# Attention plus gated MLP with its backward pass: dead buffers take wo's last rows and two O^T tiles, w_down is loaded in pieces, the guard's end and the first row tiles get a fixed place

## The chip, the cores and the metric

The kernel runs on one core of a Trainium2 chip. The number that counts is the device time in microseconds of one execution; the kernel before has a median of 5105.49 us over six runs (5099.11 to 5111.01). Lower is better. The core has a matrix engine (PE, TensorE), a vector engine (DVE), a scalar engine (ACT), a general engine (POOL, GpSimd) and a sync engine (SP), each with an instruction stream of its own. SP and POOL here mostly issue DMA transfers, each from its own queue and in the order of that queue.

## The reference

One layer, and the gradients of its inputs. With S = 2048 rows, D = 576, H = 32 heads of 128, F = 4608:

```python
xn = layernorm(x)                                   # per row
q  = (xn @ wq)  per head                            # keys and values come from caches
p  = softmax(q k^T * 128 ** -0.5)
s  = concat_heads(p @ v) @ wo
h  = sigmoid(xn @ w_gate) * (xn @ w_up)
out = x + s * silu(h @ w_down)
# returned: out and the gradients of x, k_cache, v_cache, wq, wo, w_gate, w_up, w_down
```

All tensors are bfloat16; sums are kept in float32.

## The kernel before, in words

Rows are cut into NT = 16 tiles of 128, D into five contraction tiles (DT), F into 36 (FT). The work is one long sequence of stages.

*Stage a1, norm and the first half of the MLP (lines 305 to 435).* `x_all` holds all rows. For each tile, `bn` (DVE) takes statistics, `rstd` (ACT square root, then DVE) turns those of several tiles into scale and bias, `norm` (ACT) normalizes in place, `turn` (PE) transposes into PSUM and `put_T` copies into `xnT`, the transposed xn, which is kept for the heads' queries. The weights of gate and up are loaded in five column groups (`groups1`: one of 512 columns, four of 1024). The loop runs over groups and in each over the 16 row tiles; for every 512 columns PE makes `g_ps` (L408) and `u_ps` (L410), ACT the sigmoid into `a_row` (L413), DVE the product into `h_row` (L414). `a_row` and `h_row` have four buffers each; POOL stores both per row tile (L427, L428), and a buffer is free again when its store has landed. In group 0 the norms and transposes of later tiles run two tiles ahead. After group 0 POOL stores xn (L430) and loads w_down whole (L431).

This stage lies in `tc.manual_schedule()`: on each engine the instructions written in the block keep the written order. Elsewhere a planner decides at build time, from its own estimate of when each instruction is ready, so an instruction may stand far from where it is written; instructions written after the block can also be put between those of the block.

*The guard.* `guard_load` (SP) and `guard_square` (DVE and ACT in turn) sum squares of the keys and of wq through the dead `x_all`, to choose between two softmax forms. `guard_reduce` sends two columns through DRAM into `gr`; `guard_end` (L299 to L303, five short DVE instructions) makes the flag. It is called after the block of a1.

*Stage a2 (lines 442 to 513)* multiplies h by w_down (L486), makes silu and its derivative, and transposes the gradient of s into `dsT`.

*The heads (lines 540 to 796).* Each head has 16 slots of scores (`main1`: L578, exponent L596) and 16 of gradients (`main2`: L648, L651), with work of neighbouring heads between them. `put(slot, ...)` writes a piece of work into a slot; the planner orders what is written. SP transposes every slab of probabilities (`PT`) and of their gradient (`dST`, both L572), wanted by PE (L625) five slots later. Sums over queries (L684) leave as `kvo` tiles (L696) with two buffers, stored by POOL (L698). O is stored to `on2_d` four row tiles at a time. In the last head, rows of wo are loaded into buffers that are no longer needed (`wo_parts`: dsT takes 17 heads' rows, one K buffer, V and dO three each; 26 of 32), and O^T of the first row tile goes into the dead K^T/Q^T buffer `KQ` (L532).

*Stage c1, output projection (lines 839 to 902).* The other six heads' rows of wo are loaded into `wo_x` at its start. For each row tile SP transposes that tile's rows of `on2_d` (L532) into one of two buffers (`KQ`, `oTb`), one tile ahead; PE runs 64 matmuls (L887); ACT and DVE make the gradient `doB` and the output tile `o0b`. Every two row tiles POOL loads the next `dsg`, `g2b`, `xb` and stores `o0b`. PE transposes each `doB` tile (L58) about two row tiles later. From row tile 12 on, POOL loads `ah` and SP pieces of w_down^T for the next stage. Here SP and POOL keep the written order, and memory of dead tiles is waited for tile by tile.

*The rest (stages b1, c2, c4)* makes the weight gradients and the gradient of x. `xn_all` is reloaded in b1 (L958).

Of the kernel before, what the change touches and what calls it, by code (L numbers as in the profile page):

```python
# [13 lines left out]
P = 128  # L14
# [52 lines left out]
def kernel(  # L67
# [160 lines left out]

    px = tc.alloc_tile_pool(name="px", bufs=1)
    xnT = px.tile([P, DT, S], bf, name="xnT")  # L230
    flag_i = pers.tile([1, 1], mybir.dt.int32, name="flag_i")
    with tc.tile_pool(name="pa", bufs=1) as pa:
# [75 lines left out]
        with tc.tile_pool(name="a1w", bufs=1) as wp:  # L308
# [30 lines left out]
            with tc.tile_pool(name="a0", bufs=3) as sb0, tc.tile_pool(name="a0ps", bufs=2, space=PSUM) as ps0, \  # L339
# [39 lines left out]
                for st in range(LA):  # L379
                    norm(st)  # L380
                    turn(st)
                    put_T(st, "v")
                for st in range(LA, L1):
                    bn(st)
                if LA < L1:
                    rstd(LA, L1)
                    norm(LA)
                bn_left = list(range(L1, NT))
                nstep = sum(NT * (fz - fa) for fa, fz in groups1[1:])
                ntot = len(pieces) + GLA  # L390
                step = 0
                for gi, (fa, fz) in enumerate(groups1):
                    for st in range(NT):
                        if gi == 0:
                            if st + LA + 1 < NT:
                                norm(st + LA + 1)
                            if st + LA < NT:
                                turn(st + LA)
# [3 lines left out]
                        for fc in range(fa, fz):  # L402
# [6 lines left out]
                            for i, (d0, kd) in enumerate(dts):  # L409
                                nc.tensor.matmul(u_ps[:], lhsT=xnT[:, i, srows], rhs=wu_sb[:, i, fs], start=(i == 0), stop=(i == DT - 1))  # L410
                            if gi == 0 and st + LA < NT:
                                put_T(st + LA, "s")
                            nc.scalar.activation(a_row[:, cs], g_ps[:], AF.Sigmoid)  # L413
# [13 lines left out]
                        nc.gpsimd.dma_start(h_d[srows, fa * FCH:fz * FCH], h_row[:, :nn])  # L427
                        nc.gpsimd.dma_start(a_d[srows, fa * FCH:fz * FCH], a_row[:, :nn])  # L428
                    if gi == 0:
                        nc.gpsimd.dma_start(xn_d[:, :].rearrange("(t p) d -> p t d", p=P), x_all[:])  # L430
                        nc.gpsimd.dma_start(wd_sb[:], B_w_down.rearrange("(t p) d -> p t d", p=P))  # L431
            while gk[0] < ntot:
                guard_step()
                if gk[0] == ntot:
                    guard_reduce()
            guard_end()
            NHV = min(NT, NT * D // (FT * P))
# [77 lines left out]
        gp.release()  # L515

    wo_parts = []
    for dead, t_ in enumerate((dsT, Kns[H % 2], Vn, dOn)):
        flat = t_[:].rearrange("p a b -> p (a b)")
        h0 = sum(n for _, _, n, _ in wo_parts)  # L520
        n = min(flat.shape[1] // D, H - h0)
        if n:
            wo_parts.append((flat[:, :n * D].rearrange("p (h d) -> p h d", d=D), h0, n, dead))
    n_pre = sum(n for _, _, n, _ in wo_parts)

    def load_wo_rows(dst, h0, a, b, eng=nc.gpsimd):
        eng.dma_start(dst[:, a:b, :], A_wo[(h0 + a) * P:(h0 + b) * P, :].rearrange("(h p) d -> p h d", p=P))

    oT0 = KQ[:].rearrange("p a b -> p (a b)")[:, :H * P].rearrange("p (h q) -> p h q", q=P) if H * P <= 2 * S else None

# [9 lines left out]
    def attention(fast):  # L540
        with ExitStack() as es:
# [184 lines left out]
            def q(k):  # L726
                return min(k, NT - 1)
# [46 lines left out]
            for view, h0, n, dead in wo_parts:  # L774
                for k in range(0, n, 4):
                    at = (1 + k // 4, q(skew + 1), q(skew + 2), q(skew + 4))[dead]
                    put(bl + q(at), 0, lambda view=view, h0=h0, k=k, n=n: load_wo_rows(view, h0, k, min(k + 4, n)))
            if oT0 is not None:
                put(bl + NT, 0, lambda: load_oT(oT0, 0))
            slot = 0  # L780
# [19 lines left out]
    pdT.release()  # L800
    px.release()

# [11 lines left out]
    with late("pc") as pc, late("pcw") as pcw, late("pcf") as pcf, \  # L814
# [23 lines left out]

        with late("c1w") as wp, late("c1b") as blk, late("c1l3", 2) as ldp3, late("c1s", 2) as sb, \
                late("c1ps", 2, space=PSUM) as ps, late("c1pt", 2, space=PSUM) as pst:  # L840
            wo_of = {}
            for view, h0, n, _ in wo_parts:
                for k in range(n):
                    wo_of[h0 + k] = view[:, k, :]
            if n_pre < H:
                wo_x = wp.tile([P, H - n_pre, D], bf, name="wo_x")
                load_wo_rows(wo_x, n_pre, 0, H - n_pre)
                for k in range(H - n_pre):
                    wo_of[n_pre + k] = wo_x[:, k, :]
            oTs = [oT0 if oT0 is not None else blk.tile([P, H, P], bf, name="oTa")[:], blk.tile([P, H, P], bf, name="oTb")[:]]  # L850
            if oT0 is None:
                load_oT(oTs[0], 0)
            SG1 = ldiv(NT, 2)
# [12 lines left out]
            for st in range(NT):  # L866
                if st + 1 < NT:
                    load_oT(oTs[(st + 1) % 2], st + 1)
                g, sl = divmod(st, SG1)
                if sl == 0:  # L870
                    if g + 1 < NG1:
                        groups[g + 1] = group_loads(g + 1)
                    dsg, g2b, xb = groups.pop(g)
                    o0b = ldp3.tile([P, SG1, D], bf, name="o0b")
                if st >= NT - 2 - DT and len(wd_pieces) > (F // WCH - 1) * DT:
                    wd_piece()
                if st == NT - NT // 4:
                    load_blk(ah0[:, 0, :, :], a_d, 0)
                    load_blk(ah0[:, 1, :, :], h_d, 0)
                while len(pend_tr) > 1:  # L880
                    st_ = pend_tr.pop(0)
                    transpose_to(nc, pst, doB[:, st_, :], D, doBT, st_ * P, ident, alt, eng="s")
                oT = oTs[st % 2]
                accs = [ps.tile([P, 512], f32, name=f"acc{j}") for j in range(len(ncs))]
                for h in range(H):
                    for j, (n0, nn) in enumerate(ncs):
                        nc.tensor.matmul(accs[j][:, :nn], lhsT=oT[:, h, :], rhs=wo_of[h][:, n0:n0 + nn],  # L887
                                         start=(h == 0), stop=(h == H - 1))
                s_sb = sb.tile([P, D], f32, name="s_sb")
                for j, (n0, nn) in enumerate(ncs):  # L890
                    alt.copy(s_sb[:, n0:n0 + nn], accs[j][:, :nn], eng="s")
                nc.vector.tensor_tensor(doB[:, st, :], s_sb[:], dsg[:, sl, :], op=ALU.mult)
                t0 = sb.tile([P, D], f32, name="t0")
                nc.vector.tensor_tensor(t0[:], s_sb[:], g2b[:, sl, :], op=ALU.mult)
                nc.vector.tensor_tensor(o0b[:, sl, :], t0[:], xb[:, sl, :], op=ALU.add)
                if sl == SG1 - 1:
                    nc.gpsimd.dma_start(o0[g * SG1 * P:(g + 1) * SG1 * P, :].rearrange("(t p) d -> p t d", p=P), o0b[:])
                pend_tr.append(st)
            while len(wd_pieces) > (F // WCH - 1) * DT:
                wd_piece()  # L900
            for st_ in pend_tr:
                transpose_to(nc, pst, doB[:, st_, :], D, doBT, st_ * P, ident, alt, eng="s")
        pds.release()

        def padded(pool, n, nm):
# [255 lines left out]
```

## Time and profile before

| | us |
|---|---|
| profiled execution, its own time | 5110.69 |
| its span, first to last instruction | 5108.8 |
| median of six runs (lowest, highest) | 5105.49 (5099.11, 5111.01) |
| PE busy in the span | 4989.5 |
| stage a1 | 0 to 360 |
| stage a2 | 360 to 512 |
| heads | 512 to 3704 |
| output projection c1 | 3706 to 3850 |
| rest | 3850 to 5109 |

The mean granted clock of PE is 0.992. Times in the profile are microseconds from the start of the span unless marked ns. A row of the timeline gives start, duration, engine, source line, operation and the tiles written and read; the bracket is how long the engine had been idle before it and which instruction or transfer ended that. A wait row gives the waiter, the releaser, the sum of the waits, their number and the longest. In a table of stretches each row gives the stretch, its length, PE busy time with its number of matmuls, the granted clock, the DMA share and GB/s. A busy PE is not a PE at full speed: after a pause its clock can be half, and five matmuls of 512 columns then take 2.1 us instead of 1.08.

### The profile page before, as it was taken

The page shows a single profiled execution, that of the slowest core. Times are in us where ns is not written, and L with a number is a line of the kernel's source. Part 1 is how long each engine was busy: PE and PEld are TensorE (multiplying, and loading weights), DVE is VectorE, ACT ScalarE, POOL GpSimd, SP SyncE. Part 2 cuts the span into 40 slices and gives each one's busy share as a digit, 9 for nine tenths or more (in the row PEclk, how much of TensorE's full clock was granted, in tenths as well). Part 3 has the DMA queues.
Part 4 walks back from the last instruction along what each step waited for, and adds up shares of the span by engine and source line. Part 5 has one row for each costly group of instructions (what it writes and reads, how often), then busy time and mean ns, then how long its engine had stood idle before and what let it go on. Part 6 is the DMA issues. An engine that isn't in the chain of part 4 may idle for free.

```text
span 5108.8 us, 128905 instructions
## 1 busy us (share of the span) xinstructions
PE 4989.5 (98%) x54480; PEld 3487.2 (68%) x54480; DVE 2583.3 (51%) x6704; ACT 2574.2 (50%) x4634; POOL 928.8 (18%) x1434
## 2 busy tenths in 40 slices
PE   7999999999999999999999999999999999999999
PEld 3445777787777777777777777777746666555554
DVE  4544666666566666666665666665525444200111
ACT  4431766676666666666666666666513333211000
POOL 3222111111111111111111111111112222211000
PEclk9999999999999999999999999999999999999999
DMA  8667999999999999999999999999996665797976
GB/s 285 219 182 171 212 205 204 200 210 217 193 201 209 215 203 209 198 207 207 209 208 196 205 213 205 208 201 195 214 214 192 190 188 185 221 260 187 175 141 121
DMA packets 2761921, 1031.37 MB, mean 202 GB/s; under 512 B 2664497, under 2 KB 2668722, under 8 KB 2761330
## 3 DMA queue, kind: packets, MB, share of 16 engines
q1 hardware_dynamic: 2660354, 699.97, 74.3%
q0 software_dynamic: 100976, 323.05, 19.5%
q8 instruction: 428, 7.01, 0.6%
q14 instruction: 163, 1.34, 0.1%
HBM read 175.31 MB, written 182.13 MB: 70 GB/s over the span
## 4 chain that ended last, share of the span: by engine, by line
PE 82%; issue 9%; DMA 6%; POOL 2%; DVE 2%; ACT 1%; POOLq 0%; SPq 0%; DVEq 0%; ACTq 0%
PE acc L684 14%; PE acc L625 14%; PE acc L916 13%; PE sp L578 8%; PE acc L1087 7%; PE dp L648 6%; PE acc L213 5%; PE dh L969 3%; PE acc L486 3%; PE g_ps L408 2%; PE u_ps L410 2%; DMA out_dram<-kvo 2%; PE acct L146 2%; PE acc L887 1%; DVE Pq L651 1%
## 5 line engine op out<-in xcount | busy, mean ns | idle before, releaser
L596 ACT ACTIVATE Pq<-sp 128x1024 bf16<-128x1024 f32 x1024 | 1047.0, 1023 | 317.0 <-PE sp L578 304.8
L684 PEld LDWEIGHTS <-Pq 128*128 128x128 bf16 x16384 | 1006.6, 98 | 242.1 <-issue 3.9
L655 ACT ACTIVATE t<-dp,negdelta 128x1024 bf16<-128x1024 f32 x512 | 571.1, 1115 | 222.6 <-PE dp L648 210.0
L651 DVE SCALAR_TENSOR_TENSOR Pq<-dp,negdelta,Pq 128x1024 bf16<-128x1024 f32 x512 | 655.3, 1280 | 44.3 <-PE dp L648 43.4
L648 PE MATMUL dp<-VT,dOT 128*128 128x512 bf16 x2048 | 613.9, 382 | 41.9 <-DVE Pq L651 41.8
L578 PE MATMUL sp<-KQ 128*128 128x512 bf16 x2048 | 610.1, 380 | 2.6 <-ACT Pq L596 2.5
L625 PEld LDWEIGHTS <-PT 128*128 128x128 bf16 x8192 | 502.4, 98 | 127.9 <-DMA PT<-Pq 7.0
L625 PE MATMUL acc<-Kn,dST 128*128 128x128 bf16 x8192 | 552.0, 219 | 5.6 <-DMA dST<-Pq 5.6
L625 PE MATMUL acc<-Vn,PT 128*128 128x128 bf16 x8192 | 547.5, 219 | 5.6 <-DMA PT<-Pq 5.4
L684 PE MATMUL acc<-dOn,Pq 128*128 128x128 bf16 x8192 | 547.0, 219 | 0.0
L684 PE MATMUL acc<-Qn,Pq 128*128 128x128 bf16 x8192 | 544.6, 220 | 0.0
L625 PEld LDWEIGHTS <-dST 128*128 128x128 bf16 x8192 | 492.8, 98 | 68.5 <-DMA dST<-Pq 8.1
L656 DVE TENSOR_TENSOR Pq<-t,Pq 128x1024 bf16<-128x1024 bf16 x512 | 354.3, 692 | 359.6 <-ACT t L655 352.9
L665 ACT ACTIVATE dq_n<-acc,rsc 128x128 bf16<-128x128 f32 x512 | 188.0, 367 | 340.1 <-PE acc L625 339.0
L1103 DVE SCALAR_TENSOR_TENSOR junk<-acc,xn_all 128x512 f32<-128x512 f32 (+1 forms) x32 | 13.9, 453 | 638.1 <-ACT dxn L1102 638.1
L698 POOL DMA_DIRECT2D out_dram<-kvo x256 | 140.3, 548 | 1062.8 <-DVE kvo L696 1062.8
L619 POOL DMA_DIRECT2D on_d<-o_n x128 | 97.0, 758 | 742.3 <-DVE junk L637 391.1
L971 DVE TENSOR_TENSOR du_blk<-dh,ah 128x256 bf16<-128x256 f32 x288 | 120.6, 419 | 191.5 <-PE dh L969 189.5
L696 DVE SCALAR_TENSOR_TENSOR kvo<-acc,part 128x512 bf16<-128x512 f32 x256 | 176.0, 688 | 76.0 <-DMA out_dram<-kvo 46.4
L1102 ACT ACTIVATE dxn<-acc 128x512 f32<-128x512 f32 (+1 forms) x32 | 12.8, 406 | 395.1 <-PE acc L1087 387.6
L648 PEld LDWEIGHTS <-dOT 128*128 128x128 bf16 x2048 | 163.9, 98 | 69.5 <-issue 47.5
L583 DVE TENSOR_REDUCE rs_all<-rsp 128x1 f32<-128x2 f32 x512 | 78.1, 153 | 256.0 <-ACT Pq L596 253.9
(200 smaller groups left out, 6956.5 us busy)
## 6 DMA issues: line engine op xcount, KB each, us to landing
out_dram<-kvo POOLq DMA_DIRECT2D x256, 128.0 KB, 4.1
ah<-a_d POOLq DMA_DIRECT2D x18, 1024.0 KB, 7.2
ah<-h_d POOLq DMA_DIRECT2D x18, 1024.0 KB, 9.6
du_d<-du_blk POOLq DMA_DIRECT2D x18, 1024.0 KB, 8.5
dg_d<-dg_blk POOLq DMA_DIRECT2D x18, 1024.0 KB, 10.1
h_d<-h_row POOLq DMA_DIRECT2D x64, 256.0 KB, 2.7
a_d<-a_row POOLq DMA_DIRECT2D x64, 256.0 KB, 3.5
x_all<-in_A_k_cache_dram SPq DMA_DIRECT2D x64, 256.0 KB, 3.6
```

Source lines behind the costliest of these rows:

```text
L213: nc.tensor.matmul(av[:, :CH], lhsT=w[:, i, :], rhs=srcT[:, i, cs], start=(i == 0), stop=(i == DT - 1))
L578: nc.tensor.matmul(sp[:, c * CH:(c + 1) * CH], lhsT=hs.QT[:, qt * P:(qt + 1) * P], rhs=hs.KT[:, hf * HW_ + c * CH: hf * HW_ + (c + 1) * CH ...
L596: nc.scalar.activation(Pq[:, hsl], sp[:], AF.Exp, scale=SCALE, accum_out=hs.rsp[:, hf:hf + 1])
L625: nc.tensor.matmul(hs.acc[:, 0, :], lhsT=T[:, kt, :], rhs=rhs[:, kt, :], start=(kt == 0), stop=(kt == NT - 1))
L648: nc.tensor.matmul(dp[:, c * CH:(c + 1) * CH], lhsT=hs.dOT[:, qt * P:(qt + 1) * P], rhs=hs.VT[:, hf * HW_ + c * CH: hf * HW_ + (c + 1) * C ...
L651: nc.vector.scalar_tensor_tensor(Pq[:, hsl], dp[:], hs.negdelta[:, qt:qt + 1], Pq[:, hsl], op0=ALU.add, op1=ALU.mult)
L655: nc.scalar.activation(t[:], dp[:], AF.Identity, bias=hs.negdelta[:, qt:qt + 1], scale=1.0)
L656: nc.vector.tensor_tensor(Pq[:, hsl], t[:], Pq[:, hsl], op=ALU.mult)
L665: nc.scalar.activation(hs.dq_n[:, qt % G4, :], hs.acc[:, 0, :], AF.Copy, scale=hs.rsc[:, qt:qt + 1])
L684: nc.tensor.matmul(self.tile[:, j, :], lhsT=self.slabs[qt][:, kt * P:(kt + 1) * P], rhs=self.rhs[:, qt, :], start=(qt == self.lo), stop=(q ...
L916: nc.tensor.matmul(accs[j][:, :nn], lhsT=lhs[:, st, cols], rhs=rhs[:, st, n0:n0 + nn], start=(st == 0), stop=(st == NT - 1))
L1087: nc.tensor.matmul(self.accs[sl][j][:, :nn], lhsT=ch[:, kk, sl * P:(sl + 1) * P], rhs=wT[:, k0 + kk, n0:n0 + nn], start=(self.k + kk == 0) ...
```

## The change

- `xnT` moves to the other end of SBUF and stays allocated until the end of c1. It is dead once the last head's queries are made. It takes wo's last six heads' rows and, behind them, O^T of row tile 1. `wo_x` and `oTb` are gone.
- O^T gets three buffers: `KQ`, the one in `xnT`, and one in `xn_all`, which is not yet filled in c1. Row tiles 0 and 1 are loaded in the heads' slots, 2 at the start of c1, and tile st + 2 during tile st.
- The output tile is written in place into `xb`; `o0b` is gone.
- w_down is loaded in twelve pieces of three F tiles, after the stores of every second row tile from column group 2 on; xn is stored in four pieces.
- `guard_end` is called inside the block whose order is fixed, after its last row tile.
- First row tiles: put_T of tile 1 goes to ACT; statistics and `rstd` of tiles 2 to 6 are split into 2, 3 and 4 to 6, with the norms of 2 and 3 after the first part; tile 2 is transposed after row 0's matmuls instead of before.

```diff
-    px = tc.alloc_tile_pool(name="px", bufs=1)
+    px = tc.alloc_tile_pool(name="px", bufs=1, side="right")
...
-                    put_T(st, "v")
-                for st in range(LA, L1):
-                    bn(st)
-                if LA < L1:
-                    rstd(LA, L1)
-                    norm(LA)
+                    put_T(st, "vs"[st % 2])
+                for a, b in ((LA, min(LA + 2, L1)), (min(LA + 2, L1), L1)):
+                    for st in range(a, b):
+                        bn(st)
+                    if a < b:
+                        rstd(a, b)
+                    if a == LA:
+                        for st in range(a, b):
+                            norm(st)
                 bn_left = list(range(L1, NT))
+                wd_left = list(range(0, FT, 3))
+
+                def load_wd():
+                    f0 = wd_left.pop(0)
+                    f1 = min(f0 + 3, FT)
+                    nc.gpsimd.dma_start(wd_sb[:, f0:f1, :], B_w_down[f0 * P:f1 * P, :].rearrange("(t p) d -> p t d", p=P))
...
-                            if st + LA + 1 < NT:
+                            if LA + 2 <= st + LA + 1 < NT:
                                 norm(st + LA + 1)
-                            if st + LA < NT:
+                            if st and st + LA < NT:
                                 turn(st + LA)
...
                             if gi == 0 and st + LA < NT:
+                                if st == 0:
+                                    turn(LA)
                                 put_T(st + LA, "s")
...
+                        if gi > 1 and st % 2 and wd_left:
+                            load_wd()
                     if gi == 0:
-                        nc.gpsimd.dma_start(xn_d[:, :].rearrange("(t p) d -> p t d", p=P), x_all[:])
-                        nc.gpsimd.dma_start(wd_sb[:], B_w_down.rearrange("(t p) d -> p t d", p=P))
-            while gk[0] < ntot:
-                guard_step()
-                if gk[0] == ntot:
-                    guard_reduce()
-            guard_end()
+                        for t0 in range(0, NT, 4):
+                            t1 = min(t0 + 4, NT)
+                            nc.gpsimd.dma_start(xn_d[t0 * P:t1 * P, :].rearrange("(t p) d -> p t d", p=P), x_all[:, t0:t1, :])
+                while gk[0] < ntot:
+                    guard_step()
+                    if gk[0] == ntot:
+                        guard_reduce()
+                while wd_left:
+                    load_wd()
+                guard_end()
...
+    oTs = [oT_view(KQ[:].rearrange("p a b -> p (a b)"), 0), oT_view(xnT_flat, x_used)]
...
-                    at = (1 + k // 4, q(skew + 1), q(skew + 2), q(skew + 4))[dead]
+                    at = (1 + k // 4, q(skew + 1), q(skew + 2), q(skew + 4), q(skew + 5))[dead]
...
-                put(bl + NT, 0, lambda: load_oT(oT0, 0))
+            for st in range(min(2, NT)):
+                put(bl + NT + skew * st, 0, lambda st=st: load_oT(oTs[st], st))
...
-            if n_pre < H:
-                wo_x = wp.tile([P, H - n_pre, D], bf, name="wo_x")
-                load_wo_rows(wo_x, n_pre, 0, H - n_pre)
...
+            oTs.append(oT_view(xn_all[:].rearrange("p t d -> p (t d)"), 0))
+            if NT > 2:
+                load_oT(oTs[2], 2)
...
-                if st + 1 < NT:
-                    load_oT(oTs[(st + 1) % 2], st + 1)
+                if st and st + 2 < NT:
+                    load_oT(oTs[(st + 2) % 3], st + 2)
...
-                    o0b = ldp3.tile([P, SG1, D], bf, name="o0b")
...
-                nc.vector.tensor_tensor(o0b[:, sl, :], t0[:], xb[:, sl, :], op=ALU.add)
+                nc.vector.tensor_tensor(xb[:, sl, :], t0[:], xb[:, sl, :], op=ALU.add)
...
         pds.release()
+        px.release()
```

## The prediction

> **What bounds the kernel now.** I read the busy row of the page first, then what TensorE (PE) waited for over the whole execution (waiter, releaser, total us, times, longest us):
>
> ```profile
> PE 4989.5 (98%) x54480; PEld 3487.2 (68%) x54480; DVE 2583.3 (51%) x6704; ACT 2574.2 (50%) x4634; POOL 928.8 (18%) x1434
> ...
> PE dp L648 <- DVE Pq L651: 41.8, 46, 4.6
> PE pt L369 <- ACT x_all L363: 16.5, 3, 6.9
> PE g_ps L408 <- ACT a_row L413: 10.2, 1, 10.2
> PE u_ps L410 <- DVE h_row L414: 7.3, 1, 7.3
> ...
> PE acc L887 <- DMA oTb<-on_d: 3.2, 2, 3.1
> PE acc L887 <- DMA KQ<-on_d: 2.9, 2, 2.6
> PE acc L887 <- DMA wo_x<-in_A_wo_dram: 1.9, 1, 1.9
> ```
>
> PE is busy 4989.5 of 5108.8 us, so no shorter list of matmuls is at stake; only its 119 us of pauses, and the slow matmuls after a pause, can be won. The largest row (L648, inside the heads) is not touched. The next six are what the edits aim at. I then opened the timeline at each (start, duration, instruction; in brackets the idle time before it and its releaser), and for the output projection the chain of waits:
>
> ```profile
> 13.34 0.30 ACT L355 ACTIVATE std<-mv_all,eps_t 128x5 f32<-128x5 f32 x1 [6.01 <-DVE mv_all L350]
> 19.86 0.69 DVE L414 TENSOR_TENSOR h_row<-u_ps,a_row 128x512 bf16<-128x512 f32 x1 [5.79 <-PE u_ps L410]
> 30.78 0.30 ACT L355 ACTIVATE std<-mv_all,eps_t 128x9 f32<-128x9 f32 x1 [2.87 <-DVE mv_all L350]
> 32.49 0.45 PE L369 MATMUL pt<-ident,x_all 128*128 128x128 bf16 x5 [2.99 <-ACT x_all L363]
> ...
> 63.96 1.83 POOL L431 DMA_DIRECT2D wd_sb<-in_B_w_down_dram  x1
> 92.34 0.54 POOL L428 DMA_DIRECT2D a_d<-a_row  x1 [12.84 <-DMA wd_sb<-in_B_w_down_dram]
> 93.87 1.08 ACT L413 ACTIVATE a_row<-g_ps 128x512 bf16<-128x512 f32 x2 [16.45 <-DMA a_d<-a_row]
> 94.52 2.29 PE L408 MATMUL g_ps<-wg_sb,xnT 128*128 128x512 bf16 x5 [10.17 <-ACT a_row L413]
> ...
> 340.38 0.27 DVE L299 TENSOR_REDUCE gs<-gr 1x1 f32<-1x128 f32 x1 [12.33 <-DMA gr<-gd_d]
> 342.09 2.29 PE L410 MATMUL u_ps<-wu_sb,xnT 128*128 128x512 bf16 x5 [7.29 <-DVE h_row L414]
> 347.75 1.24 PE L408 MATMUL g_ps<-wg_sb,xnT 128*128 128x512 bf16 x5
> ...
> 3727.76 8.20 DMA oTb<-on_d
> 3818.06 15.88 DMA KQ<-on_d
> ```
>
> **A, first rows.** Now the standard deviations of tiles 2 to 6 come at once (13.34), tile 2 is transposed ahead of row 0, and row 0's `h_row` starts at 19.86. DVE then alternates three or two statistics (0.95 us a tile) with an `h_row` until std 7 to 15 at 30.78, 10.9 us later, and tile 7's transpose waits for that (32.49). In the new order row 0 needs only put_T(0), done at 7.9, and its weights, whose landings I read from the tile's own view (issue 2.7 + 5.8 = 8.5; `wu` 4.0 + 6.5 = 10.5). Gate and up run at the half clock of the first matmuls, 2.1 us each, to 12.7. DVE does bn 2 and 3 from 7.9, 0.4 us of rstd, bn 4 to 6 to 13.6; ACT then std 0.3, put_T(2) 0.7, the table load 1.3, sigmoid 0.6: `h_row` at about 16.6. The same 10.9 us chain follows, so tile 7 comes 3.2 us earlier, and PE is bound by itself from there. PE gets ahead and only waits longer at tile 7: of the 5 to 7 us that row 0 starts earlier, 3.2 remain. Bounds 2 and 4.
>
> **B, w_down in pieces.** One 5184 KB load sits in POOL's queue before the row stores. The store issued at 66.57 lands at 93.8, so `a_row`'s fourth buffer is not free and PE, due at 84.18, starts at 94.52. The next two groups run slow, and the third starts at 98.31 where, at the 1.08 us of an undisturbed group, 84.18 + 2 x 1.08 = 86.34 was due: 12.0 us. After the edit only xn (2304 KB, 10.5 us to land) is ahead of these stores; they land near 76, and the buffer is wanted at 81. POOL's issue there stays 3.0 us: four xn issues of about 0.75 (the row of a 576 KB load) against 1.17 + 1.83. Guard loads on SP may start near 66 instead of 73.5, adding some 1.3 MB by 81: (2.86 + 1.3) MB at 300 GB/s still ends at 77. The twelve pieces go behind the stores of odd rows in groups 2 and 3, 0.7 us of POOL each where POOL is idle 3.2 us a row. The Trainium skill speaks against this: its page "DMA: Bandwidth & Descriptors" wants transfers of 1 MiB or more (section "Measured (HBM→SBUF, 128 partitions, SWDGE, issued from GpSimd)"), and its fit of 2.0 us plus bytes over 436 GB/s (section "Anatomy of one DMA — SWDGE (gpsimd) path") makes 14.2 us of one load and an estimated 12 x 3.0 = 36 us of twelve. The row for the single load is 27.9 us among other traffic, and the count that matters is PE's: from 130 to 325 us DMA moves 211 GB/s, against 378 from 80 to 100, so 5.3 MB over 100 us (53 GB/s) fits, and the first use is at 359.9. By the rule's time the load is 22 us longer and still ends 100 us early; I take 12.0 (bounds 9 and 12.2, the lower one with a leftover pause at 81).
>
> **C, guard's end.** DVE sat 12.33 us in front of L299 for a small DMA, with `h_row` queued behind it. PE groups: g at 333.57, undisturbed rhythm again at 347.75, three groups later; 347.75 - (334.65 + 3 x 1.08) = 9.9 us. Pinned behind the last `h_row`, its five instructions take 1.0 us (340.38 to 341.35) while DVE has nothing until 369.6. The DMA landed at 340.3, some 20 us before that `h_row`; all of that shifts together. 9.9, bounds 9 and 10.
>
> **D, output projection.** From 3706.48 to the first L969 at 3850.43 are 143.9 us. A row without waits is 7.84 us, 14 rows carry transposes of 0.28: 129.4. Excess 14.6: wo_x 2.1, transposes placed ahead of row 1 and waiting for doB 1.7, row 0's slow clock 1.3, the rest O^T: a reload needs 8.2 us against a row of 8.12, and 11.5 and 15.9 us where `ah` loads run beside it. With three buffers a reload is issued two rows (16.2 us) ahead, which covers even 15.9; wo's last six rows and the second O^T are loaded during the last head. What remains is the slow clock. The Trainium skill's "TensorE: Matmul & The Clock Gate" (Part 1, the HAM clock gate) lets the clock fall after an idle window of about 3.4 us; by that the 2.82 us pause at the branch would cost nothing and the gain be 14.6. The row decides: granted clock 0.72 and 0.81 just after it.
>
> ```profile
> 3704.00:3708.00 4.00, 1.52 (x7) 0.72 0.51 128
> 3708.00:3711.00 3.00, 3.00 (x23) 0.81 1.35 292
> ```
>
> So at most 13.3; some waits of a few tenths will stay: 12.8. Low bound 8: the doB wait stays (1.7) and row 15 meets the `ah` loads (3.1). The new wait is for xb: it is now the output, so its next load waits on POOL for the store before it to land (4.3 us). Behind it stand `ah`, at row 12 (wanted 25 us later), and the next store; neither is late. At the end of D, dg_blk or ah1 may now lie on xb and wait for the last store to land, 3.3 us of DVE; the layout is not in the trace: 0 to 3, I take 1.
>
> **E, what moves into the last head.** wo's pieces went out as soon as their buffer was dead (dsT's at 3602, 13 slots before their place), so I expect xnT's 864 KB at about 3587, and O^T 1 on SP after on_d's first store (3617.2), not where it is written. It takes 4.7 to 6.2 us of SP among transposes of 2.1 us in slots of 3.4; behind it wait PT 9 to 12, each wanted five slots (17 us) after its slab. O^T 0 did the same at 3643.73 and cost PE 0.33 us. The dsT loads made one PT take 15.1 us and PE wait 5.1, and stay. Bounds 0 and 6; nearest is O^T 0: 1.5. If xnT frees late, the loads slip and D loses at most 2.1.
>
> **Sum.** 3.2 + 12.0 + 9.9 + 12.8 - 1.0 - 1.5 = 35.4 us. The profiled execution took 5110.7 us (span 5108.8 and 1.9 around it), giving 5075; the six runs have a median of 5105.5, and 5105.5 - 35.4 = 5070.
>
> **Rivals.** *Waits move (0.13).* One or two pauses come back in another place: the stores still late behind xn and earlier guard loads, O^T at rows 13 to 15, PT in the last head. For it: DMA is at 0.84 to 1.04 in those stretches. Against: the slacks above. It costs 9 to 18 us: 5079 to 5088. *The change doesn't do what it says (0.05).* The code outside the pinned block was moved around by its planner, and SP's order is not seen: O^T 1 issued only in its written slot, and the guard's DMA late. Gains A and B alone remain: 5090. *The heads get worse (0.12).* PE in an undisturbed head window is busy 97.76 of 98; some 13 of 32 stall, for 49 us less 9 in the last. There DVE waits 45.8 us for `kvo` stores to land, two buffers deep. These heads come in groups every 590 to 700 us, like a beat between head and something else, and all heads will start 25 us earlier and with other slab addresses. A stalled head costs 40/13 = 3.1 us; gains are used up when 11 more stall, and if all do, 19 x 3.1 = 59 us: 5129. Past 8 more it is no gain that can be told, past 15 it is slower. Against it: no instruction of these heads changes, and the groups recur evenly whatever came before. *The plan holds (0.70):* 5060 to 5080.
>
> **Numbers.** A difference under 0.2% (10 us) can't be told from none here. Faster: 0.70 + 0.13 + 0.05 = 0.88, since the plan and the first two rivals all end over 10 us below; of the heads' 0.12, 0.05 is the stretch from 8 to 15 more stalls (same) and 0.07 what lies past it (slower). Range 5055 to 5092: below, upper bounds (4 + 12.2 + 10 + 13.3, no losses, 39.5) and a few stalled heads less; above, the first two rivals.
>
> **What would show it.** A: std of nine tiles at about 27.6, tile 7's transpose near 29.3. B: no PE pause over 1 us between 60 and 100. C: L299 after the last `h_row`. D: L887 stretch 131 us, no wo_x row, no O^T wait over 1 us. E: PE waits for PT and dST in the last head at most 11 us. Wrong if PE's wait for L651 leaves 35 to 50 us, or if a new row over 5 us stands in PE's waits.

## The result and the profile after

The changed kernel takes 5083.97 us (median of 19 runs, 5064.88 to 5105.44); the kernel before, run beside it, 5104.26 us (40 runs, 5087.22 to 5118.64). The ratio is 0.9958 with a 95% interval of 0.9948 to 0.9967: 20.3 us faster, between 16.8 and 26.5. The forecast was 5070, in a range of 5055 to 5092. Sign and range held; the gain came out at little more than half of the 35.4 us of the sum.

The profiled execution alone would have hidden that. It took 5075.18 us (span 5073.3, mean granted clock 0.993), 35.5 less than the one of before, as if the sum had been right to a tenth. But it lies 8.8 under its kernel's median, and the one of before 6.4 over its own. The experiments show which terms of the sum were right and which this one execution flattered.

First the page's busy row of the changed kernel, its row for the `kvo` tiles, and what PE waited for over the whole execution (waiter, releaser, total us, times, longest us):

```profile
PE 4983.4 (98%) x54480; PEld 3487.1 (69%) x54480; DVE 2583.5 (51%) x6705; ACT 2575.0 (51%) x4636; POOL 938.8 (19%) x1449
...
L718 DVE SCALAR_TENSOR_TENSOR kvo<-acc,part 128x512 bf16<-128x512 f32 x256 | 176.0, 687 | 69.6 <-DMA out_dram<-kvo 34.4
...
PE dp L670 <- DVE Pq L673: 34.5, 47, 3.5
PE acc L647 <- DMA PT<-Pq: 14.1, 3, 6.8
PE pt L369 <- ACT x_all L363: 13.9, 3, 6.6
PE acc L647 <- DMA dST<-Pq: 4.2, 5, 1.5
...
PE acc L902 <- DMA out_dram<-kvo: 2.8, 1, 2.8
```

The rows for the MLP's sigmoid and product (10.2 and 7.3 us before) are gone, and so is every row for O^T and `wo_x`. L670, the largest, is the kernel's old L648 and stays. One row grew by more than 1 us: PE's wait for `PT`, 5.4 us before, is now 14.1, all of it in the last head. Before, the rows for the `kvo` tiles and for `PT` were

```profile
L696 DVE SCALAR_TENSOR_TENSOR kvo<-acc,part 128x512 bf16<-128x512 f32 x256 | 176.0, 688 | 76.0 <-DMA out_dram<-kvo 46.4
...
PE acc L625 <- DMA PT<-Pq: 5.4, 2, 5.1
```

The timeline at the places that the prediction opened:

```profile
16.13 0.69 DVE L426 TENSOR_TENSOR h_row<-u_ps,a_row 128x512 bf16<-128x512 f32 x1 [2.10 <-ACT a_row L425]
...
27.09 1.28 ACT L355 ACT_TABLE_LOAD   x1 [5.50 <-DVE mv_all L350]
28.39 0.30 ACT L355 ACTIVATE std<-mv_all,eps_t 128x9 f32<-128x9 f32 x1
30.10 0.72 PE L369 MATMUL pt<-ident,x_all 128*128 128x128 bf16 x5 [5.71 <-ACT x_all L363]
...
61.33 3.00 POOL L446 DMA_DIRECT2D xn_d<-x_all  x4
...
335.53 0.69 DVE L426 TENSOR_TENSOR h_row<-u_ps,a_row 128x512 bf16<-128x512 f32 x1 [1.48 <-PE u_ps L420]
336.14 0.26 DVE L299 TENSOR_REDUCE gs<-gr 1x1 f32<-1x128 f32 x1
```

Row 0's product starts 3.7 us earlier, tile 7's transpose 2.4 us earlier, behind a longer pause (5.71 instead of 2.99). The guard's end stands directly behind the last `h_row` and waits for nothing. Between 60 and 100 us PE is busy in every one of four stretches of 10 us (stretch, length, PE busy time with matmuls, weight loads, DVE, ACT, POOL, granted clock, DMA share, GB/s); the last two, where the pause had been, read

```profile
80.00:90.00 10.00, 10.00 (x48) 4.54 (x47) 5.57 (x9) 4.75 (x9) 2.14 (x4) 1.00 0.69 257
90.00:100.00 10.00, 10.00 (x48) 4.51 (x46) 5.22 (x9) 4.30 (x8) 3.04 (x6) 1.00 0.60 210
```

By stage, from the first matmul of each line: the MLP ends (L503 begins) at 336.3 instead of 359.9, 23.6 us earlier; the heads take 3195.9 instead of 3194.7; the projection (stage c1) 131.3 instead of 143.9; what follows 1257.9 instead of 1258.4.

### The profile page after: what moved, and what is told of

Its sections match the earlier page's. It is cut to its first block, busy times and chain, and to the rows that moved or that the text cites. A ratio compares the mean times of both kernels' runs of the same rounds, so it can differ in the third digit from the quotient of the medians.

```text
span 5073.3 us, 128938 instructions
## 1 busy us (share of the span) xinstructions
PE 4983.4 (98%) x54480; PEld 3487.1 (69%) x54480; DVE 2583.5 (51%) x6705; ACT 2575.0 (51%) x4636; POOL 938.8 (19%) x1449
## 4 chain that ended last, share of the span: by engine, by line
PE 86%; issue 7%; DMA 3%; DVE 2%; POOL 1%; ACT 1%; POOLq 0%; DVEq 0%; ACTq 0%
PE acc L706 15%; PE acc L647 15%; PE acc L932 13%; PE sp L600 8%; PE acc L1103 7%; PE dp L670 7%; PE acc L213 5%; PE u_ps L420 3%; PE g_ps L418 3%; PE dh L985 3%; PE acc L902 3%; PE acc L503 2%; PE acct L146 2%; DMA out_dram<-kvo 2%; DVE Pq L673 1%
## 5 line engine op out<-in xcount | busy, mean ns | idle before, releaser
L673 DVE SCALAR_TENSOR_TENSOR Pq<-dp,negdelta,Pq 128x1024 bf16<-128x1024 f32 x512 | 655.3, 1280 | 44.9 <-PE dp L670 43.9
L670 PE MATMUL dp<-VT,dOT 128*128 128x512 bf16 x2048 | 614.0, 382 | 34.6 <-DVE Pq L673 34.5
L647 PE MATMUL acc<-Vn,PT 128*128 128x128 bf16 x8192 | 548.3, 219 | 14.2 <-DMA PT<-Pq 14.1
L1118 ACT ACTIVATE dxn<-acc 128x512 f32<-128x512 f32 (+1 forms) x32 | 12.8, 406 | 394.9 <-PE acc L1103 387.4
L718 DVE SCALAR_TENSOR_TENSOR kvo<-acc,part 128x512 bf16<-128x512 f32 x256 | 176.0, 687 | 69.6 <-DMA out_dram<-kvo 34.4
L50 DVE TENSOR_SCALAR o_n<-acc,rinv_all 128x128 bf16<-128x128 f32 x352 | 123.3, 350 | 169.7 <-PE acc L647 169.7
```

Source lines behind the costliest of these rows:

```text
L647: nc.tensor.matmul(hs.acc[:, 0, :], lhsT=T[:, kt, :], rhs=rhs[:, kt, :], start=(kt == 0), stop=(kt == NT - 1))
L670: nc.tensor.matmul(dp[:, c * CH:(c + 1) * CH], lhsT=hs.dOT[:, qt * P:(qt + 1) * P], rhs=hs.VT[:, hf * HW_ + c * CH: hf * HW_ + (c + 1) * C ...
L673: nc.vector.scalar_tensor_tensor(Pq[:, hsl], dp[:], hs.negdelta[:, qt:qt + 1], Pq[:, hsl], op0=ALU.add, op1=ALU.mult)
```

## The experiments

The stages are read from profiled executions throughout: the start of a2's matmuls, the heads, the projection from its first matmul to the first L985, and the rest. All medians are set against runs of the kernel before on the same chip.

### The change again, and its heads without the stall (e1, e2, e3)

The first run is the changed kernel again. The other two take a stall out of the way that both kernels have: DVE waits for `kvo` stores to land, which is what PE's L670 row is. Both kernels got four buffers instead of two:

```diff
-                            fo_ = stg.tile([P, 4, P], bf, name="kvo")
+                            fo_ = stg.tile([P, 4, P], bf, name="kvo", bufs=4)
```

> The changed kernel once more, to see what differs between its executions. Theory T (the gain outside the heads is fixed at 36 to 37 us and the heads vary): against the profile of the changed kernel the stretch up to the first score matmul and the stretch from the first L902 on agree within 1 us, and the whole difference in time lies between, in PE's waits at L670 for DVE and at L647 for PT. Rival U (a part of the gain in the MLP or the output projection is lost in some executions): one of the two outer stretches is 3 us or more longer in this profile. Time 5074 to 5095 by both.

> The changed kernel with four kvo buffers instead of two, nothing else. Theory T: PE's waits at L670 for DVE L673 (34.5 us) fall under 10 us, the kernel is 25 to 45 us faster than the changed one (about 5045), and its times scatter less. Rival V (these waits come from DVE being late for another reason): no gain over 5 us, the waits stay over 30 us.

> The kernel before with four kvo buffers. Theory T: the difference to the changed kernel with four kvo buffers is then the fixed gain less what the last head loses, 36.5 - 8.7 = 28 us (24 to 32), because the waits that scatter are gone in both; 30 to 40 us faster than the kernel before. Rival W (the change itself makes the heads worse by something other than kvo): the difference stays near the measured 20 us or less. Rival V: same as the kernel before.

| | median us | lowest to highest | ratio to before, 95% |
|---|---|---|---|
| changed, again | 5083.31 | 5058.86 to 5101.55 | 0.9960 (0.9946 to 0.9975) |
| changed, four kvo buffers | 5045.21 | 5038.81 to 5054.44 | 0.9887 (0.9868 to 0.9906) |
| before, four kvo buffers | 5064.53 | 5062.23 to 5071.91 | 0.9925 (0.9909 to 0.9941) |

With the stall gone the change is still worth 19.3 us. So the gap between 35.4 and 20 isn't made by the heads' stores: the rival that put it there falls. With it falls what I expected of e1 and e3, a fixed gain outside the heads that only the heads' waits hide: 24 to 32 us should have been left between e3 and e2, and in e1 the stretch from the first L902 on lasts 1394.3 us against 1389.2 in the result's profile, where I had allowed 1. The largest waits of the changed kernel with four buffers:

```profile
PE acc L647 <- DMA PT<-Pq: 10.2, 4, 4.8
PE dp L670 <- DVE Pq L673: 7.8, 32, 0.4
PE acc L647 <- DMA dST<-Pq: 7.5, 9, 1.4
PE acc L902 <- DMA KQ<-on_d: 6.7, 1, 6.7
```

L670 falls from 34.5 to 7.8, a residue of 0.24 us for each of 32 heads. And there is a row that the profile of the result lacks: the projection waited 6.7 us for an O^T tile; in e1 it waited 3.7. Both are at the same place, row tile 3. The SP and POOL rows of the changed kernel with four buffers there:

```profile
3646.16 0.72 POOL L876 DMA_DIRECT2D dsg<-dsg_d  x1 [8.10 <-DMA out_dram<-kvo]
3646.86 0.73 POOL L876 DMA_DIRECT2D g2b<-g_d  x1
3647.59 0.70 POOL L876 DMA_DIRECT2D xb<-in_A_x_dram  x1
3648.28 0.72 POOL L876 DMA_DIRECT2D dsg<-dsg_d  x1
3648.57 14.09 SPq L554 DMA_TRANSPOSE KQ<-on_d  x1
3649.00 0.70 POOL L876 DMA_DIRECT2D g2b<-g_d  x1
3649.69 0.72 POOL L876 DMA_DIRECT2D xb<-in_A_x_dram  x1
...
3671.48 0.66 PE L902 MATMUL acc<-dsT,KQ 128*128 128x512 bf16 x2 [6.71 <-DMA KQ<-on_d]
```

Six group loads of 288 KB stand around the first reload of an O^T buffer. Undisturbed the reload occupies SP for 4.7 us; here it takes 14.09 and lands 22.9 after its issue, more than the lead of two rows (16.2 us) that the prediction gave it. In e1 it was 13.33, in the result's profile 8.22 (landing at 11.8, no wait): the same code, met at a slightly different moment (the last of the six loads is issued 0.15 us ahead of the reload there, 0.5 us behind it in e1 and 1.1 behind it here).

### The change in two halves (e4, e5)

e4 is the kernel before with the MLP's edits alone (first rows, w_down and xn in pieces, guard's end). e5 is the kernel before with the rest alone (`xnT` kept, wo's last rows in it, three O^T buffers, output in `xb`), with four kvo buffers; its base is therefore e3.

> The kernel before with only the MLP stage's edits (first rows, w_down and xn in pieces, guard's end pinned). Theory T: 23.6 us earlier at the first score matmul, the heads as in the kernel before, so 21 to 25 us faster; PE's waits for PT stay at about 5 us. If instead the heads' groups of stalls are moved by a start 24 us earlier, the gain is under 15 us and the waits at L648 for L651 grow over 50 us.

> The kernel before with the change's edits of the output projection alone (wo's last rows in xn^T, second and third O^T buffer, the wo loads of the last head), and with four buffers for the kvo staging, so that its base is the kernel before with four kvo buffers: ratio 0.9925, 5064.5 us. My prediction's terms D, -1.0 and E sum to a gain of 11.3: 5053 us. Theory N (the projection part nets nothing): the stage of O^T rows is 8 us shorter, not 12.8, since the first reload of an O^T buffer meets the six group loads of dsg, g2b and xb, and the last head is 8 us longer: 5064.5, within 4 of its base. If N holds, PE's waits for PT in the last head stand at 9 to 14 us and the stage of L902's matmuls at 138 to 141 us.

e4: 5083.78 us (5072.72 to 5085.44), ratio 0.9952 (0.9935 to 0.9969). The MLP half alone gives 21.4 us, as expected (21 to 25), and all that the whole change gives. e5: 5064.37 us (5058.29 to 5066.54), ratio 0.9923 (0.9910 to 0.9937), against 0.9925 for its base: the projection half nets nothing that can be told from zero. My terms for this half sum to 10.3 us (12.8 - 1.0 - 1.5; the 11.3 of the expectation leaves out the 1.0). They would have made a ratio of about 0.9905, a little below e5's interval. In its profile the projection takes 139.3 us (148.4 in e3), and the last head lost what that won: PE waits 10.4 us for `PT` there instead of 5.3.

Over all executions profiled, before the change or with the MLP half alone (three), the projection takes 141.8 to 148.4 us, mean 144.7. In the eight with both the three buffers and O^T 1 in the last head and `wo` in its place (the changed kernel, e1, e2, e5, e7, e9, e10, e11) it takes 131.3 to 143.4, mean 136.4: 8.3 gained (the first four of them, which carry no edit to this part, have the same mean, 136.5). The last head, from the first load of wo rows into `dsT` to the first matmul of the projection, takes 102.9 to 104.8 us without these edits (mean 103.9) and 107.8 to 113.4 with them (mean 110.1): 6.2 lost.

### Why the first reload is late (e7), and O^T 1 out of the last head (e6, e8)

e7 moves the second group's loads behind the first group's store; e6 loads O^T 1 at the start of the projection; e8 does both. All have four kvo buffers. The edit of e7, then that of e6:

```diff
-                    if g + 1 < NG1:
+                    if g and g + 1 < NG1:
...
+                    if g == 0:
+                        groups[1] = group_loads(1)
```

```diff
-            for st in range(min(2, NT)):
-                put(bl + NT + skew * st, 0, lambda st=st: load_oT(oTs[st], st))
+            put(bl + NT, 0, lambda: load_oT(oTs[0], 0))
...
+            load_oT(oTs[1], 1)
             if NT > 2:
                 load_oT(oTs[2], 2)
```

> The changed kernel with four kvo buffers (5045.2 us), with the three loads of the second group of dsg, g2b and xb moved behind the store of the first group's xb, so that three and not six group loads stand beside the first reload of an O^T buffer. If the collision with group loads makes that reload late, its transpose issues in 5 to 9 us instead of 14, PE's wait for it at row 3 falls from 6.7 to under 2 us, and the projection takes 131 to 134 us instead of 140: 5037 to 5040 us. If the reload is slow for another reason (the buffer's place, the transposes before it on SP), it stays at 13 to 14 us of issue and 5045.

> The changed kernel with four kvo buffers (5045.2 us in the run of that name), with one thing more: O^T 1 is loaded at the start of the output projection, beside O^T 2, and not in the last head. If O^T 1's load is what delays the last head's PT transposes, the last head loses only what the wo rows cost: PT waits fall from 10 to 5 us and the heads are 4 to 6 us shorter, 3146 to 3148 against 3151.5. If the two wo loads are the cause, the PT waits stay at 9 to 11 us and the heads at 3151. In the projection SP then issues two O^T transposes one after the other before the first reload: row 1 needs O^T 1 some 8 us after row 0 begins, so it waits 0 to 4 us for it, and the first reload comes 5 us later still. Sum: 5040 to 5048.

> Both edits together: the second group's loads behind the first group's store, and O^T 1 loaded at the start of the projection. If the two causes are separate, the gains add: heads 3146 to 3148 and projection 131 to 136, 5033 to 5039. If O^T 1 at the projection's start only moves the wait there (row 1 waits for it), it is no better than the edit of the groups alone: 5038 to 5043.

| | median us | ratio to before, 95% | heads | projection |
|---|---|---|---|---|
| e2, base | 5045.21 | 0.9887 (0.9868 to 0.9906) | 3151.5 | 140.1 |
| e7 | 5036.20 | 0.9885 (0.9867 to 0.9903) | 3150.3 | 131.3 |
| e6 | 5040.40 | 0.9871 (0.9852 to 0.9890) | 3147.8 | 143.2 |
| e8 | 5039.39 | 0.9875 (0.9858 to 0.9892) | 3152.8 | 140.6 |

The total times don't tell these kernels apart. The profiles do. SP and POOL of e7 at the first reload:

```profile
3645.64 0.72 POOL L876 DMA_DIRECT2D dsg<-dsg_d  x1 [8.02 <-DMA out_dram<-kvo]
3646.34 0.73 POOL L876 DMA_DIRECT2D g2b<-g_d  x1
3647.07 0.70 POOL L876 DMA_DIRECT2D xb<-in_A_x_dram  x1
3648.34 5.40 SPq L554 DMA_TRANSPOSE KQ<-on_d  x1
...
3659.40 0.72 POOL L912 DMA_DIRECT2D out_dram<-xb  x1 [11.62 <-DVE xb L910]
3660.12 0.70 POOL L876 DMA_DIRECT2D dsg<-dsg_d  x1
```

The same transpose, at the same place behind the same transposes, takes 5.40 us of SP instead of 14.09 and lands in 8.9 instead of 22.9: the three loads issued beside it were the cause. e9 and e10, which carry the same edit, show 5.51 and 5.58 us. The distance counts as well as the number: in e11, which also carries it, the first of the three loads came 0.7 us ahead of the reload and the other two behind it, and it took 8.54 us and landed in 17.2. PE waits for no O^T tile in e7. In e6 and e8 the reload of row 3 was quick as well (5.24 and 5.22): row 0 ran later there, so the last group load was 5 to 8 us ahead of it. But PE waited 10.1 and 7.0 us at row 15. Waits of e6 and its SP and POOL rows there:

```profile
PE acc L902 <- DMA KQ<-on_d: 10.1, 1, 10.1
PE acc L902 <- DMA out_dram<-kvo: 7.3, 1, 7.3
PE acc L647 <- DMA PT<-Pq: 5.2, 2, 4.2
```

```profile
3743.94 12.69 SPq L554 DMA_TRANSPOSE KQ<-on_d  x1
3744.50 1.16 POOL L847 DMA_DIRECT2D ah<-a_d  x1
3745.65 1.15 POOL L847 DMA_DIRECT2D ah<-h_d  x1
```

The last reload is issued 0.56 us ahead of the two `ah` loads (1 MB each) and takes 12.69 us of SP; it lands 26.5 us after its issue. In the result's profile it is issued 2.3 us ahead of them, takes 4.83 and lands in 10.3: PE doesn't wait. Before, the reload beside the `ah` loads was that of row 14 (13.61, landing 15.9) and cost 2.6 us; a third buffer doesn't cover such a reload when the two start together.

Loading O^T 1 at the projection's start also delays the start: the first matmul waits 7.3 and 8.4 us for the last `kvo` stores instead of 2.6 to 2.8, beside two O^T transposes instead of one. So e8 got neither of the two gains that I expected to add up (heads of 3146 to 3148, projection of 131 to 136). Which place of O^T 1 is better isn't shown: heads and projection together take 3291.0 us in e6 and 3291.6 in e2, but 3293.4 in e8 and 3281.6 in e7, one execution each.

### The guard's end, w_down and the first rows, each undone (e9, e10, e11)

The base is e7 (5036.2 us, a2 begins at 336.4). It ran on another chip, where the kernel before had 5101.22 us and not 5103.54. Set against the kernel before, e9, e10 and e11 have ratios of 0.9901, 0.9897 and 0.9867 and e7 has 0.9885, each within about 0.002, so the times alone don't show these terms; the start of a2 in the profiles does.

```diff
                 while wd_left:
                     load_wd()
-                guard_end()
+            guard_end()
```

```diff
-                        if gi > 1 and st % 2 and wd_left:
-                            load_wd()
...
+                        wd_left.clear()
+                        nc.gpsimd.dma_start(wd_sb[:], B_w_down.rearrange("(t p) d -> p t d", p=P))
```

e11 turns back all lines of the first row tiles, as the diff of the change shows them.

> The changed kernel with four kvo buffers and the second group of loads late (5036.2 us, its L503 matmuls begin at 336.4), with the guard's end back outside the block whose order is pinned. My term C (9.9, bounds 9 to 10): the pause for the guard's broadcast comes back ahead of the last rows of the MLP, L503 begins at 345.5 to 346.5 and the time is 5045 to 5047. Rival: the order on the queues is the same without the pin, since the guard's data come at another time now; then 336.4 and 5036.

> The same base, with w_down loaded whole behind the pieces of xn's store after the first group of columns, as in the kernel before, and not in pieces. My term B (12.0, bounds 9 to 12.2): the pause between 60 and 100 us comes back, L503 begins at 345 to 348.6 and the time is 5045 to 5048. Rival: the store of xn in four pieces alone keeps the stores of h and a on time, so that no more than half of the pause comes back: L503 at 336.4 to 342.

> The same base, with the first row tiles in the order of the kernel before. My term A (3.2, bounds 2 to 4): L503 begins 3.2 later, at 339.6. From the traces of before and after I now read 1.4 to 1.5 of it, since a table load on ScalarE that lay in a wait now delays the square roots and TensorE stays at half clock longer: 337.9. The time 5037 to 5040 in either case, which is less than it scatters.

| undone | a2 begins | later by | median us (lowest to highest) |
|---|---|---|---|
| guard's end pinned (e9) | 346.7 | 10.3 | 5046.56 (5038.57 to 5076.51) |
| w_down in pieces (e10) | 349.3 | 12.9 | 5050.00 (5038.97 to 5053.84) |
| first rows (e11) | 336.9 | 0.5 | 5036.80 (5033.79 to 5040.31) |

Both pauses return where they were. e9, DVE:

```profile
327.08 0.27 DVE L299 TENSOR_REDUCE gs<-gr 1x1 f32<-1x128 f32 x1 [12.83 <-DMA gr<-gd_d]
```

e10, POOL's queue and PE's wait:

```profile
63.55 1.83 POOL L446 DMA_DIRECT2D wd_sb<-in_B_w_down_dram  x1
...
91.79 0.54 POOL L440 DMA_DIRECT2D a_d<-a_row  x1 [14.49 <-DMA wd_sb<-in_B_w_down_dram]
...
PE g_ps L418 <- ACT a_row L425: 11.1, 1, 11.1
```

xn's store is in pieces in e10 and the pause is whole: it is w_down's single load that holds the stores of `h` and `a` up, not xn's. The reordered first rows are worth 0.5 us, no more than a2's start differs between executions of the same MLP code (335.4 to 337.3 in eight of them); the 10.3 and 12.9 us are clear of that.

### What lengthens the last head (e12)

The base is e7; wo's last six rows go into `xnT` at the start of the projection, O^T 1 stays.

```diff
-            for view, h0, n, dead in wo_parts:
+            for view, h0, n, dead in wo_parts[:4]:
...
+            for view, h0, n, dead in wo_parts[4:]:
+                for k in range(0, n, 4):
+                    load_wo_rows(view, h0, k, min(k + 4, n))
```

> The same base, with wo's last six rows loaded into xn^T at the start of the output projection and not in the last head; O^T 1 stays in the last head. The stretch of the last head between the loads of wo into dsT and into Vn takes 53.9 to 55.5 us without the change's edits and 58.0 to 63.6 with them. If O^T 1 is what lengthens it, it stays at 58 to 62 here; if the xn^T rows do, it falls to 54 to 56. In the projection row 0 then waits for the six rows, as the kernel before waited for wo_x, or longer since two loads of 864 KB in all stand beside the first group's: 3 to 8 us. Time 5036 to 5046.

5035.62 us (5030.30 to 5044.34), ratio 0.9863 (0.9846 to 0.9879). From the first `dsT` load to the `Vn` load:

```profile
3526.12 1.50 POOL L545 DMA_DIRECT2D dsT<-in_A_wo_dram  x2 [4.87 <-PE acc L213]
...
3587.24 0.75 POOL L545 DMA_DIRECT2D Vn<-in_A_wo_dram  x1 [6.91 <-PE acc L647]
```

That is 61.1 us, as long as with the rows loaded early (58.0 to 63.6), so the `xnT` rows are not what lengthens it. Without O^T 1 in the last head the same stretch took 54.1 us in e6 (54 to 55.5 before the change) but 60.8 in e8, where PE waited 5.78 us behind the `dsT` loads and 3.12 behind O^T 0. So O^T 1 is the likelier cause but not the only one; two executions that disagree don't settle it. Row 0 of e12 waits 4.9 us for its rows, as the kernel before waited for `wo_x`, and row 15 waits 7.3 us for a reload issued 0.4 us ahead of the `ah` loads (projection 147.3).

### The best version

The changed kernel with four kvo buffers beats both kernels clearly: 5045.2 us, and 5035.6 to 5036.8 in the three variants e7, e11 and e12, at ratios of 0.9863 to 0.9885 to the kernel before, against 0.9958 for the change. Between these variants nothing can be told by time.

## Why the prediction was right, and where it was not

| term | predicted | measured | from |
|---|---|---|---|
| A, first rows | 3.2 | 0.5, not told from 0 | e11 |
| B, w_down in pieces | 12.0 | 12.9 | e10 |
| C, guard's end | 9.9 | 10.3 | e9 |
| D, output projection | 12.8 | 8.3 | means of 3 and 8 executions |
| layout wait at D's end | -1.0 | 0 | rest 1258.4 and 1257.9 |
| E, last head | -1.5 | -6.2 | means of 3 and 8 executions |
| sum | 35.4 | 25.8 | 20.3 (16.8 to 26.5) between the medians |

Sign and range held because of B and C, 21.9 of the 35.4 us. A, D and E fell short by 2.7, 4.5 and 4.7, and the range had room for that. The sum of the measured terms is 5.5 us above the difference of the medians, inside its interval; A, B and C are read from one execution each, and which of the five is too large isn't shown.

**B and C** were right in mechanism, place and size, each a little over its upper bound (12.2 and 10). B was also the part that a rule spoke against; the twelve 432 KB loads cost PE nothing, since the question was never how long w_down takes but what stands behind it in POOL's queue.

**A** failed at the step "tile 7 comes 3.2 us earlier, and PE is bound by itself from there". Tile 7 came 2.4 earlier: the table load for the square root (1.28 us of ACT) ran before at 26.63, while the statistics were not yet there; in the new order it starts only when they are, at 27.09, so the nine standard deviations come at 28.39 and not 27.6. Then PE is not bound by itself: its pause ahead of tile 7 is 5.71 us instead of 2.99, and it comes out of it slower. The stretches from 28 to 36 us, before and then after (columns as above):

```profile
28.00:32.00 4.00, 1.49 (x7) 0.49 (x5) 3.02 (x11) 0.74 (x2) 1.07 (x2) 1.00 1.04 357
32.00:36.00 4.00, 3.51 (x14) 1.48 (x15) 0.69 (x1) 3.97 (x6) 0.06 (x1) 0.63 1.04 352
```

```profile
28.00:32.00 4.00, 1.90 (x9) 1.08 (x10) 0.38 (x2) 3.48 (x6) 0.00 (x0) 0.58 1.04 372
32.00:36.00 4.00, 4.00 (x16) 1.82 (x15) 1.38 (x2) 3.46 (x6) 1.07 (x2) 0.56 1.05 324
```

The granted clock reads 1.00 and 0.63 before, 0.58 and 0.56 after, and of the 2.4 us 1.5 are left when row tile 6 begins (35.41 instead of 36.90). I charged the pause and left out the clock behind it, though D's working had just used that effect. The size also differs between executions: in e7, the base of e11, tile 7's transpose starts at 31.17, 0.6 us earlier than in e11.

**D** failed at "With three buffers a reload is issued two rows (16.2 us) ahead, which covers even 15.9". The 15.9 was the longest landing in one execution, not a bound. Reloads landed in up to 26.5 us where plain loads ran beside them: at row 3 with the six group loads, at row 15 with `ah`. The result's profiled execution was one of three in eight where PE waited for neither (131.3 us each), and its 12.6 agree with the term for that reason only. Row 3 waited in e1, e2 and e5, rows 14 and 15 in e9, row 15 in e11. The lower bound of 8 named row 15; that the mean lies there is partly chance, since row 3 makes as much of it. Row 3 I had not seen: before, row 0 lasted 13.2 us, so the first reload was issued 4.7 us behind the last of the six group loads, landed in 8.5 us and was not waited for. The 8.3 are good to some 5 us only, estimated from the spread of the executions (141.8 to 148.4 in three, 131.3 to 143.4 in eight). The wait of the next `xb` load on its store (4.3 predicted) was 2.4 to 5.2 us in the two profiles of the changed kernel, up to 7.8 in e2, and delayed nobody that I could find.

**E** failed at "nearest is O^T 0: 1.5". The order was right: `xnT` rows early, O^T 1 among the `PT` transposes, not where it is written. PE's waits for `PT` and SP's rows in the changed kernel:

```profile
3592.86 1.89 PE L647 MATMUL acc<-Vn,PT 128*128 128x128 bf16 x16 [6.81 <-DMA PT<-Pq]
...
3600.66 4.98 SPq L554 DMA_TRANSPOSE xnT<-on_d  x1
...
3611.27 1.07 PE L647 MATMUL acc<-Vn,PT 128*128 128x128 bf16 x16 [2.67 <-DMA PT<-Pq]
...
3620.91 5.34 SPq L554 DMA_TRANSPOSE KQ<-on_d  x1
...
3632.32 1.89 PE L647 MATMUL acc<-Vn,PT 128*128 128x128 bf16 x16 [4.58 <-DMA PT<-Pq]
```

Before, O^T 0 came 41 us after the `dsT` loads and cost 0.33 us. Now the `dsT` loads, O^T 1 and O^T 0 come 30 and 20 us apart, and each takes its price out of the same lead of `PT` over PE; the second and third find it used. That reading is argued from these rows; shown is the size, 6.2 us, just past my upper bound of 6. PE's waits for `PT` and `dST` in this head were 12.4 to 16.8 us in the changed kernel's first two executions, where I had promised at most 11.

**The rivals.** The outcome is my rival of waits that move (5079 to 5088) by its own list: "O^T at rows 13 to 15, PT in the last head". I gave it 0.13 and the plan 0.70, because I took slacks from one execution as if they held in all. The heads did not get worse: their stall for stores went from 46.4 to 34.4 us of DVE time, and the difference with it removed in both (19.3) is that of the plain kernels (20.3). Of my signs of being wrong, PE's wait for DVE in the heads (L651, now L673) left its 35 to 50 us, if only just and on the good side: 34.5, and 31.2 in e1. A new row over 5 us stands in no profile of the changed kernel itself (the `PT` row grew from 5.4 to 14.1); with four `kvo` buffers there is one, the 6.7 us for O^T.

## What to carry to other kernels

Before a slack is called cover, ask what else is issued just before the transfer or with it; a landing seen once is a sample, not a bound. When several small delays are moved in front of one consumer, price them together against its one lead, not each by its own row. And where an engine's wait is moved, look at what was hidden inside it (a table load, a cold clock): it becomes visible in the new place.

## What was unexpected of the hardware

- A DMA transpose that is issued close to plain loads from another queue lands late. The last O^T reload shows it with two loads of 1 MB (`ah`). Issued 1.7 to 3.6 us ahead of the first of them it took 4.8 to 6.2 us of SP and landed in 10.3 to 12.1 (the changed kernel, e1, e2, e5, e7, e10). Issued 1.3 us ahead it landed in 20.3 (e11), and 0.4 to 0.6 us ahead in 23.5 to 26.5 (e6, e8, e12). The time on SP alone doesn't tell: it was 12.69 and 14.84 us in e6 and e12, but 6.24 in e8. Issued 2 to 6 us behind them, the reload of row 14 or 15 took 10.4 to 13.6 us of SP and landed in 12.8 to 15.9 (before, e3, e4, e9). Among six loads of 288 KB the first reload took 13.1 to 14.1 us and landed in 19.9 to 22.9 (e1, e2, e5), and in the result's profile 8.22 and 11.8. Even three loads were enough when they came 0.7 us before it (e11: 8.54 us, landing 17.2; there the load of `xb` was late as well and held DVE up for 7.61 us).
- A pause of 2.6 to 2.8 us in front of the projection lowered PE's granted clock over the next 8 us in some executions (0.79 in the changed kernel, e1, e5, e7, e9 and e10; 0.83 before and in e2) and not in others (1.00 in e3, e4, e11, e12). The Trainium skill's "TensorE: Matmul & The Clock Gate" (Part 1, the HAM clock gate) says that the clock watches free-running windows of some 3.4 us and falls after an idle one. A free-running window would explain that equal pauses count or don't by where they fall, which no run here shows. That it takes a whole idle window the runs contradict: a pause shorter than one was enough in eight of twelve.
